# The second half of a layer's columns in one pass: loads by two experts, and four outputs after the last product

## The chip, the core and the metric

The kernel runs on one core of a Trainium2 chip. The core has a matrix engine (TensorE, PE in the rows, with PEld for its weight loads), three engines for elementwise work (VectorE or DVE, ScalarE or ACT, GpSimd or POOL), an engine that issues transfers (SyncE, SP), and 16 DMA engines that move data between the device memory and the on-chip memory. Matrix products are written to PSUM, a small memory that DVE and ACT read out. The metric is device time in microseconds of one execution, lower is better.

## What is computed

An attention between 512 tokens and 32 states of 8 batches and 8 heads gives 8 x 544 rows of 512 columns; a soft mixture of experts follows. Its second half is what matters here:

```python
logits = x @ phi                                  # 4608 rows, 8 experts x 4 slots
d = softmax(logits, over rows);   slot_input = (d.T @ x).reshape(E, 4, 512)
for e in range(8):
    h = np.maximum(slot_input[e] @ w1[e], 0.0)    # 4 x 1024
    slot_out[e] = h @ w2[e]                       # 4 x 512: the second layer
c = softmax(logits, over the 32 slots)
return c @ slot_out                               # 4608 x 512
```

All numbers are 32-bit floats. w1 and w2 are 16 MB each, the output is 9 MB.

## The kernel before

The first part, the attention and the sums over all rows, follows an order written out by hand (ORDER), and is the same in both kernels. After it the kernel runs the first layer of the experts (`w1_part`, h_ps), then the second layer, then the outputs.

**The second layer in column pieces.** The 512 columns of w2 are made in pieces. Columns 0 to 255 are one piece, `wide_part`, whose sum stands in the PSUM tile so[0]; columns 256 to 383 and 384 to 511 are two pieces of 128, `w2_part` with k = 2 and 3, in so[2] and so[3]. For each piece `part` runs over two halves hf of the 1024 hidden features and over 8 experts e: 4 matmuls each, one for each 128 features, into 4 groups of 32 partitions that run side by side. `so_copy(k)` takes the finished piece out of PSUM (ACT the first 128 columns, DVE the rest), `so_sum(k)` adds the 4 groups with a matmul by `rep`, and ACT copies the sum to so_r.

**The outputs.** `out(k, q)` makes 128 of the 512 output columns (k = 0 to 3) for half of the tokens (q): 4 matmuls of so_r with the softmax weights lt_all, 4 copies into a 1 MB tile, by ACT and DVE in turn, and one DMA from SP's queue. `out_by_batches` does the same for (3, 0) in two halves of 512 KB, in PSUM tiles of 256 columns. `out_st(k)` makes 128 columns for the state rows; after each second one a 256 KB DMA, out_s, is issued.

**The order.** The code's order is the order on each engine. At the end (from line 887) small parts stand between the outputs: `more(n)` runs the next n of 32 parts of 128 columns, first all 16 of k = 2, then those of k = 3. out(0, 0) to out(1, 1) need the first piece alone, out(2, *) need k = 2, and out(3, *) need k = 3.

**Loads.** All loads from the third batch on and all outputs go through SP's one queue, in order of issue; SP waits for the buffer of a transfer before it issues it, and for the eighth transfer before it. `load_w` takes weights from a list `todo`. The columns 256 to 511 come in four loads of 2 MB (L117), each with 128 columns of 4 experts; between the second and the third is one load for the first piece, `last`. They use the four `pairs` buffers that the first layer's weights leave. The four are issued before the first layer's second half is done.

Of the kernel before, what the change touches and what calls it, by code (L numbers as in the profile page):

```python
# [8 lines left out]
F32 = mybir.dt.float32  # L9
# [6 lines left out]
P = 128  # L16
# [4 lines left out]
E = 8  # L21
F = 1024
NJ = S // P
# [40 lines left out]
def attention_soft_moe(ctx: ExitStack, tc: tile.TileContext, x0, x1, x, st0, st1, phi, w1, w2a, w2b, out_x, out_s):  # L64
# [6 lines left out]
    nc = tc.nc  # L71
    pe, act, dve, pool = nc.tensor, nc.scalar, nc.vector, nc.gpsimd
# [3 lines left out]
    big = ctx.enter_context(tc.tile_pool(name="big", bufs=NBIG))  # L76
    pairs = ctx.enter_context(tc.tile_pool(name="pairs", bufs=NPAIR))
# [6 lines left out]
    for b in range(B):  # L84
        t = big.tile([P, 4, NJ, 2 * D], F32, tag="big", name=f"x{b}")
# [18 lines left out]
    w1t, w2t = {}, {}  # L104
    todo = [(1, hf, e) for hf in range(2) for e in range(E)]
    todo += [(2, k, e) for k in range(2) for e in range(0, E, 2)]
    last = todo.pop()
    todo += [(3, 0, 0), (3, 0, 4), last, (3, 1, 0), (3, 1, 4)]
    both = []

    def load_w(n):
        for _ in range(min(n, len(todo))):
            layer, k, e = todo.pop(0)
            if layer == 3:
                t = pairs.tile([P, 4 * F], F32, tag="pair", name=f"w3_{k}_{e}")
                t = t.rearrange("p (e k f) -> p e k f", e=4, k=8)
                nc.sync.dma_start(t, w2b[e // 4, k])  # L117
                for i in range(32):
                    w2t[3, k, e + i // 8, i % 8] = t[:, i // 8, i % 8]
                continue  # L120
            if layer == 1 and len(w1t) < 8 * NPAIR:
                if not both:
                    t = pairs.tile([P, 4 * F], F32, tag="pair", name=f"w1_{k}_{e}")
                    both.extend((t[:, 0 : 2 * F], t[:, 2 * F :]))
                t = both.pop(0)
            else:
                t = big.tile([P, 2 * F], F32, tag="big", name=f"w{layer}_{k}_{e}")
            if layer == 1:
                t = t.rearrange("p (k f) -> p k f", k=4)
                nc.sync.dma_start(t, w1[k, e])  # L130
                for i in range(4):
                    w1t[k, e, i] = t[:, i]
            else:
                t = t.rearrange("p (e k f) -> p e k f", e=2, k=4)
                nc.sync.dma_start(t, w2a[e // 2, k])
                for i in range(8):
                    w2t[layer, k, e + i // 4, i % 4] = t[:, i // 4, i % 4]
# [30 lines left out]
    lt_all = cp.tile([P, B, P], F32, name="lt_all")  # L168
# [8 lines left out]
    with ExitStack() as actx:  # L177
        wk = actx.enter_context(tc.tile_pool(name="work", bufs=1))
        sm = actx.enter_context(tc.tile_pool(name="small", bufs=2))
        ps_s = actx.enter_context(tc.tile_pool(name="ps_s", bufs=2, space=PSUM))  # L180
        ps_t = actx.enter_context(tc.tile_pool(name="ps_t", bufs=3, space=PSUM))
        ps_m = actx.enter_context(tc.tile_pool(name="ps_m", bufs=3, space=PSUM))
# [10 lines left out]
        def half(name):  # L193
            return wk.tile([P, S], F32, tag="h", name=name, bufs=NH)

        def mtile(shape, name):
            return ps_m.tile(shape, F32, tag="ms", name=name)
# [467 lines left out]
        def SIe():  # L665
# [5 lines left out]
            E=E_, ee=ee, A=A_, ae=ae, R=R_, sr=sr, srT=srT, srTe=srTe, Lx=Lx, keep=keep, mx=mx, mk=mk,  # L671
# [85 lines left out]
        so, so_sb, so_r = {}, {}, {}  # L757

        def part(k, hf, e, cols, w):
            if hf == 0 and e == 0:  # L760
                so[k] = ps_s.tile([P, cols], F32, tag="sc", name=f"so_ps{k}")
            for i in range(4):
                pe.matmul(  # L763
                    so[k][32 * i : 32 * i + 32, :],
                    h_m[hf][:, 256 * i + 32 * e : 256 * i + 32 * e + 32],
                    w(i),
                    start=(hf == 0 and e == 0),
                    stop=(hf == 1 and e == E - 1),
                )
# [1 line left out]
        def wide_part(hf, e):  # L771
            part(0, hf, e, 256, lambda i: w2t[2, hf, e, i])

        def w2_part(k, hf, e):
            part(k, hf, e, P, lambda i: w2t[3, k - 2, e, 4 * hf + i])

        def so_copy(k):
            cols = so[k].shape[1]
            so_sb[k] = half(f"so_sb{k}")[:, 0:cols]
            act.copy(so_sb[k][:, 0:P], so[k][:, 0:P])  # L780
            if cols > P:
                dve.tensor_copy(so_sb[k][:, P:cols], so[k][:, P:cols])

        def so_sum(k, half_of=0):
            c = slice(P * half_of, P * half_of + P)
            p = mtile([P, P], f"sum_ps{k}_{half_of}")
            pe.matmul(p, rep, so_sb[k][:, c], start=True, stop=True)
            i = k + half_of
            if i % 2 == 0:
                so_r[i // 2] = half(f"so_r{i // 2}")[:, 0:256]  # L790
            act.copy(so_r[i // 2][:, P * (i % 2) : P * (i % 2) + P], p)

        def out(k, q):
            hf, col = k // 2, 128 * (k % 2)
            o = [(ps_t if j % 2 else ps_m).tile([P, 512], F32, tag="tr" if j % 2 else "ms", name=f"o{k}_{q}_{j}")
                 for j in range(NJ)]
            for j in range(NJ):
                rows = slice(32 * j, 32 * j + 32)
                pe.matmul(  # L799
                    o[j],  # L800
                    so_r[hf][rows, col : col + 128],
                    lt_all[rows, 4 * q : 4 * q + 4, :].rearrange("p b s -> p (b s)"),
                    start=True,
                    stop=True,
                )
            ot = big.tile([P, NJ, 512], F32, tag="big", name=f"out{k}_{q}")
            for jp in range(2):
                act.copy(ot[:, 2 * jp, :], o[2 * jp])  # L808
                dve.tensor_copy(ot[:, 2 * jp + 1, :], o[2 * jp + 1])  # L809
            nc.sync.dma_start(out_x[k, q], ot)  # L810

        def out_by_batches(k, q):
            hf, col = k // 2, 128 * (k % 2)
            homes = ((ps_m, "ms"), (ps_t, "tr"), (ps_m, "ms"), (ps_t, "tr"), (ps_s, "sc"), (ps_t, "tr"), (ps_s, "sc"), (ps_m, "ms"))
            o = [h.tile([P, 256], F32, tag=tag, name=f"o{k}_{q}_{i}") for i, (h, tag) in enumerate(homes)]
            ot = big.tile([P, 2, NJ, 256], F32, tag="big", name=f"out{k}_{q}")
            to = out_x[k, q].rearrange("p j s -> (p j s)").rearrange("(i p j s) -> i p j s", i=2, p=P, j=NJ)
            for i in range(2):
                b = 4 * q + 2 * i
                for j in range(NJ):  # L820
                    rows = slice(32 * j, 32 * j + 32)
                    pe.matmul(
                        o[4 * i + j],
                        so_r[hf][rows, col : col + 128],
                        lt_all[rows, b : b + 2, :].rearrange("p b s -> p (b s)"),
                        start=True,
                        stop=True,
                    )
            for i in range(2):
                for jp in range(2):  # L830
                    act.copy(ot[:, i, 2 * jp], o[4 * i + 2 * jp])
                    dve.tensor_copy(ot[:, i, 2 * jp + 1], o[4 * i + 2 * jp + 1])
                nc.sync.dma_start(to[i], ot[:, i])

        ot = []

        def out_st(k):
            rows = slice(32 * k, 32 * k + 32)
            o = mtile([P, 256], f"os{k}")
            pe.matmul(  # L840
                o,
                so_r[k // 2][rows, P * (k % 2) : P * (k % 2) + P],
                lts_all[rows].rearrange("p k i n -> p (k i n)"),
                start=True,
                stop=True,
            )
            if k % 2 == 0:
                ot.append(half(f"out_s{k // 2}"))
            act.copy(ot[-1][:, 256 * (k % 2) : 256 * (k % 2) + 256], o)
            if k % 2:  # L850
                nc.sync.dma_start(out_s[k // 2], ot[-1])
# [26 lines left out]
        for e in range(E):  # L878
            wide_part(1, e)

        rest = [(k, hf, e) for k in (2, 3) for hf in range(2) for e in range(E)]

        def more(n):
            for _ in range(n):
                w2_part(*rest.pop(0))

        so_copy(0)
        more(1)
        so_sum(0)
        more(1)  # L890
        so_sum(0, 1)
        out(0, 0)
        more(5)
        out(0, 1)
        more(5)
        out(1, 0)
        more(4)
        so_copy(2)
        out(1, 1)
        so_sum(2)  # L900
        more(4)
        out_st(0)
        out_st(1)
        out(2, 0)
        more(6)
        out(2, 1)
        more(6)
        so_copy(3)
        out_st(2)
        so_sum(3)  # L910
        out_by_batches(3, 0)
        out_st(3)
        out(3, 1)

# [33 lines left out]
```

## Time and profile before

| what | value |
|---|---|
| median of three runs | 130.05 us (129.82 to 130.21) |
| span of the profiled execution, first to last instruction | 128.2 us |
| TensorE busy in it | 117.7 us (92%) |
| DVE, ACT, POOL busy | 86.7, 76.9, 44.8 us |
| moved by DMA | 51.74 MB, mean 404 GB/s |
| mean granted TensorE clock | 0.980 of full speed |
| last TensorE instruction ends | 120.7 us |

The execution's own time is not listed beside its span; the median of the runs is 1.85 us above the span, and this stands for what lies around it. Shares and rows below are of the one profiled execution, times in microseconds from the start of its span. "Landing" is the time at which the last part of a transfer has reported its end. A transfer is spread over the 16 DMA engines, and the DMA share of a stretch is the mean of the 16; it can go a little above 1 in a short stretch, since a packet is counted where it ends or begins.

### The profile page before, as it was taken

What the parts mean: (1) busy time and instruction counts of PE and PEld (TensorE: products, weight loads), DVE (VectorE), ACT (ScalarE), POOL (GpSimd) and SP (SyncE); (2) the same over time, 40 slices, a digit from 0 to 9 for tenths busy, and PEclk for the clock granted to TensorE, in tenths of its full rate; (3) what the DMA queues carried; (4) which work ended last, traced back from release to release, by engine and by line L of the source; (5) the groups of instructions that cost most, each with busy time, mean ns of one, the idle gap of its engine ahead of it and who ended that gap; (6) DMA issues with size and microseconds to landing.
All of it is one profiled execution on the core that took longest, in us unless ns stands there. A gap on an engine that the chain in (4) does not pass through costs nothing.

```text
span 128.2 us, 4700 instructions
## 1 busy us (share of the span) xinstructions
PE 117.7 (92%) x1992; PEld 81.7 (64%) x1992; DVE 86.7 (68%) x194; ACT 76.9 (60%) x189; POOL 44.8 (35%) x63
## 2 busy tenths in 40 slices
PE   5999999999999999999999999999999999998600
PEld 2857686789795869768767769953465655575200
DVE  2329999999999999999985669019830356442600
ACT  4039999999999999999965711310100436645600
POOL 3004366391947467467882105703500000000000
PEclk9999999999999999999999999999999999999965
DMA  4999999999999999999999999999999989999992
GB/s 125 377 407 430 424 427 422 424 422 424 422 419 422 427 419 429 419 429 417 429 417 435 412 420 402 459 440 409 412 445 445 389 366 417 429 406 422 385 423 100
DMA packets 8373, 51.74 MB, mean 404 GB/s; under 512 B 928, under 2 KB 1184, under 8 KB 3360
## 3 DMA queue, kind: packets, MB, share of 16 engines
q1 hardware_dynamic: 8064, 50.93, 95.5%
q10 hardware_dynamic: 288, 0.52, 1.1%
q8 instruction: 15, 0.25, 0.7%
q14 instruction: 6, 0.05, 0.1%
HBM read 42.53 MB, written 8.91 MB: 401 GB/s over the span
## 4 chain that ended last, share of the span: by engine, by line
PE 71%; DVE 9%; DMA 7%; ACT 5%; issue 1%; POOL 0%; ACTq 0%; DVEq 0%; POOLq 0%
PE so_ps L763 12%; PE h_ps L700 11%; PE xt_ps L229 8%; PE o L799 7%; PE sc L248 5%; DMA phi_sb<-phi_in 5%; PE eT_ps L312 4%; PE sr_ps L346 4%; PE an_ps L312 3%; PE lt L381 3%; DMA x<-x_in 3%; PE t_ps L506 2%; DVE sums L277 2%; DVE q L261 2%; DVE m L266 1%
## 5 line engine op out<-in xcount | busy, mean ns | idle before, releaser
L270 POOL TENSOR_TENSOR q<-q,m 128x512 f32<-128x512 f32 x16 | 16.8, 1050 | 15.7 <-DVE m L266 7.3
L234 ACT ACTIVATE xt<-xt_ps 128x512 f32<-128x512 f32 x30 | 17.9, 618 | 5.9 <-PE xt_ps L229 5.7
L229 PE MATMUL xt_ps<-ident,x 128*128 128x128 f32 x128 | 19.3, 293 | 0.0
L288 POOL TENSOR_TENSOR q<-q,rr 128x512 f32<-128x512 f32 x16 | 16.5, 1051 | 5.1 <-DVE rr L283 3.6
L229 PEld LDWEIGHTS xt_ps<-ident,x 128*128 128x128 f32 x128 | 15.5, 151 | 3.1 <-PE sc L248 0.8
L763 PE MATMUL so_ps<-w,h_m 128*32 128x128 f32 (+1 forms) x384 | 15.7, 310 | 0.0
L763 PEld LDWEIGHTS so_ps<-w,h_m 128*32 128x32 f32 x384 | 10.7, 110 | 7.4 <-issue 4.6
L809 DVE COPY out<-o 128x512 f32<-128x512 f32 x14 | 9.2, 688 | 9.0 <-PE o L799 8.8
L700 PE MATMUL h_ps<-w,si_m 128*32 128x512 f32 x128 | 14.4, 594 | 0.1
L299 DVE TENSOR_REDUCE nm<-sc 128x1 f32<-128x512 f32 x16 | 10.6, 670 | 2.7 <-PE sc L248 2.7
L808 ACT COPY out<-o 128x512 f32<-128x512 f32 x14 | 7.7, 588 | 6.8 <-PE o L799 6.7
L700 PEld LDWEIGHTS h_ps<-w,si_m 128*32 128x32 f32 x128 | 9.1, 110 | 3.9 <-issue 2.9
L304 ACT ACTIVATE e<-sc,nm 128x512 f32<-128x512 f32 x16 | 11.3, 711 | 0.4 <-DVE nm L299 0.3
L261 DVE STREAM_TRANSPOSE q<-sc 128x512 f32<-128x512 f32 x16 | 11.1, 695 | 0.1
L293 DVE STREAM_TRANSPOSE aT<-q 128x512 f32<-128x512 f32 x16 | 10.9, 689 | 0.3 <-POOL q L288 0.2
L266 DVE TENSOR_REDUCE m<-q 128x16 f32<-128x512 f32 x16 | 10.5, 659 | 0.0
L277 DVE TENSOR_REDUCE sums<-q 128x16 f32<-128x512 f32 x16 | 10.4, 664 | 0.1
L273 ACT ACTIVATE q<-q 128x512 f32<-128x512 f32 x16 | 10.4, 650 | 0.1
L346 PE MATMUL sr_ps<-x,eT 128*32 128x64 f32 x512 | 10.4, 220 | 0.0
L312 PE MATMUL eT_ps<-ident,e 128*128 128x128 f32 x64 | 9.8, 279 | 0.0
L248 PE MATMUL sc<-xt,stT_sb 64*32 64x512 f32 x128 | 9.8, 601 | 0.0
L346 PEld LDWEIGHTS sr_ps<-x,eT 128*32 128x32 f32 x512 | 8.6, 110 | 1.3 <-issue 0.8
(124 smaller groups left out, 186.1 us busy)
## 6 DMA issues: line engine op xcount, KB each, us to landing
w<-w_in SPq DMA_DIRECT2D x16, 1024.0 KB, 19.7
w<-w2b_in SPq DMA_DIRECT2D x4, 2048.0 KB, 14.7
out_x<-out SPq DMA_DIRECT2D x7, 1024.0 KB, 6.0
x<-x_in SPq DMA_DIRECT2D x6, 1024.0 KB, 13.5
w<-w2a_in SPq DMA_DIRECT2D x6, 1024.0 KB, 19.4
x<-x_in SPq DMA_DIRECT2D x2, 512.0 KB, 5.9
w<-w2a_in SPq DMA_DIRECT2D x2, 512.0 KB, 12.4
w<-w2a_in SPq DMA_DIRECT2D x4, 256.0 KB, 14.4
```

Of the source, the lines that this page charges most:

```text
L229: pe.transpose(p[:, P * j : P * j + P], xb[b][:, g, j, :], ident)
L234: act.mul(r[f"xt{g}"], r[f"xp{g}"], 0.125)
L248: pe.matmul(r[f"sp{h}"][32 * g : 32 * g + 32, :], st_t(b, g)[64 * h : 64 * h + 64, :], r[f"xt{g}"][64 * h : 64 * h + 64, :], start=True, s ...
L261: dve.transpose(r[f"q{h}"], r[f"sp{h}"])
L266: dve.tensor_reduce(out=r[f"m1{h}"], in_=r[f"qv{h}"], axis=AX.X, op=ALU.max)
L270: pool.tensor_tensor(v, v, R[b][f"m1{h}"].broadcast_to([P, 16, NS]), op=ALU.subtract)
L277: dve.tensor_reduce(out=v, in_=R[b][f"qv{h}"], axis=AX.X, op=ALU.add)
L288: pool.tensor_tensor(v, v, r.broadcast_to([P, 16, NS]), op=ALU.mult)
L312: pe.transpose(p[:, j, :], r[f"{src}{h}"][:, P * j : P * j + P], ident)
L346: pe.matmul(r["srp"][32 * g : 32 * g + 32, h, :], r[f"eT{h}"][:, j, 32 * g : 32 * g + 32], xb[b][:, g, j, D * h : D * h + D], start=(j == ...
L700: pe.matmul(h_ps[hf][32 * kt : 32 * kt + 32, :], si_m[kt // 2][:, 256 * (kt % 2) + 32 * e : 256 * (kt % 2) + 32 * e + 32], w1t[hf, e, kt], ...
L763: pe.matmul(so[k][32 * i : 32 * i + 32, :], h_m[hf][:, 256 * i + 32 * e : 256 * i + 32 * e + 32], w(i), start=(hf == 0 and e == 0), stop=( ...
```

## The change

The columns 256 to 511 become one piece of 256 columns, as the first half is. Its four loads of 2 MB hold two experts each with all 256 columns, instead of four experts with 128. Its 16 parts of 256 columns run expert by expert, both halves of the features of an expert in turn, so that they use the loads in their order. The first four outputs stand between the parts, after 2, 5, 8 and 10 of them; all 16 parts come before `so_copy(2)`, and out(2, 0), out(2, 1), out(3, 0) and out(3, 1), 1 MB each, follow the two sums of the second piece. `out_by_batches` is gone: out(3, 0) is made by `out`, in one transfer. out_st(0) and out_st(1) come ahead of the sums, out_st(2) and out_st(3) ahead of the last output.

```diff
-    todo += [(3, 0, 0), (3, 0, 4), last, (3, 1, 0), (3, 1, 4)]
+    todo += [(3, 0, 0), (3, 0, 2), last, (3, 0, 4), (3, 0, 6)]
...
             if layer == 3:
-                t = pairs.tile([P, 4 * F], F32, tag="pair", name=f"w3_{k}_{e}")
-                t = t.rearrange("p (e k f) -> p e k f", e=4, k=8)
-                nc.sync.dma_start(t, w2b[e // 4, k])
-                for i in range(32):
-                    w2t[3, k, e + i // 8, i % 8] = t[:, i // 8, i % 8]
+                t = pairs.tile([P, 4 * F], F32, tag="pair", name=f"w3_{e}")
+                t = t.rearrange("p (e k f) -> p e k f", e=2, k=8)
+                nc.sync.dma_start(t, w2b[e // 2])
+                for i in range(16):
+                    w2t[3, e + i // 8, i % 8] = t[:, i // 8, i % 8]
...
-        def w2_part(k, hf, e):
-            part(k, hf, e, P, lambda i: w2t[3, k - 2, e, 4 * hf + i])
+        def second_part(hf, e):
+            part(2, hf, e, 256, lambda i: w2t[3, e, 4 * hf + i])
...
-        rest = [(k, hf, e) for k in (2, 3) for hf in range(2) for e in range(E)]
+        rest = [(hf, e) for e in range(E) for hf in range(2)]
...
         out(0, 0)
-        more(5)
+        more(3)
         out(0, 1)
-        more(5)
+        more(3)
         out(1, 0)
-        more(4)
+        more(2)
+        out(1, 1)
+        more(6)
         so_copy(2)
-        out(1, 1)
-        so_sum(2)
-        more(4)
         out_st(0)
         out_st(1)
+        so_sum(2)
+        so_sum(2, 1)
         out(2, 0)
-        more(6)
         out(2, 1)
-        more(6)
-        so_copy(3)
+        out(3, 0)
         out_st(2)
-        so_sum(3)
-        out_by_batches(3, 0)
         out_st(3)
         out(3, 1)
```

The array w2b is laid out on the host to match, 16 KB for each partition of a load in both kernels.

On TensorE, from out(1, 1) to out(2, 0): before, with so_ps the products, sum_ps the sums, os those of out_st and o those of out (h_m_1665 and h_m_1666 are the two halves of the hidden features, so_r_1877 and so_r_2002 the two halves of the columns):

```order
L799 MATMUL o_1_0_1986<-lt_all,so_r_1877 128x512
L799 MATMUL o_1_1_1987<-lt_all,so_r_1877 128x512
L799 MATMUL o_1_2_1988<-lt_all,so_r_1877 128x512
L799 MATMUL o_1_3_1989<-lt_all,so_r_1877 128x512
L787 MATMUL sum_ps_0_2000<-so_sb_1984,rep 128x128
L763 MATMUL so_ps_2004<-w_1_0_1731,h_m_1665 32x128 x16
L840 MATMUL os_2021<-lts_all,so_r_1877 128x256
L840 MATMUL os_2025<-lts_all,so_r_1877 128x256
L799 MATMUL o_0_0_2029<-lt_all,so_r_2002 128x512
L799 MATMUL o_0_1_2030<-lt_all,so_r_2002 128x512
L799 MATMUL o_0_2_2031<-lt_all,so_r_2002 128x512
L799 MATMUL o_0_3_2032<-lt_all,so_r_2002 128x512
```

and in the changed kernel, from the last of out(1, 1)'s matmuls on (so_r_2011 is the second half of the columns):

```order
L799 MATMUL o_1_3_1963<-lt_all,so_r_1877 128x512
L763 MATMUL so_ps_1870<-w_4_1731,h_m_1665 32x256 x4
L763 MATMUL so_ps_1870<-w_4_1731,h_m_1666 32x256 x4
L763 MATMUL so_ps_1870<-w_6_1733,h_m_1665 32x256 x4
L763 MATMUL so_ps_1870<-w_6_1733,h_m_1666 32x256 x4
L763 MATMUL so_ps_1870<-w_6_1733,h_m_1665 32x256 x4
L763 MATMUL so_ps_1870<-w_6_1733,h_m_1666 32x256 x4
L817 MATMUL os_2001<-lts_all,so_r_1877 128x256
L817 MATMUL os_2005<-lts_all,so_r_1877 128x256
L787 MATMUL sum_ps_0_2009<-so_sb_1998,rep 128x128
L787 MATMUL sum_ps_1_2013<-so_sb_1998,rep 128x128
L799 MATMUL o_0_0_2016<-lt_all,so_r_2011 128x512
```

Ahead of out(2, 0) stood one sum, four small parts of the third piece and out_st; now the last six wide parts, out_st and both sums stand there.

On ACT, at the same place, before (so_sb is the copy of so_copy, so_r that of the sum):

```order
L780 COPY so_sb_1984<-so_ps_1870 128x128
L808 COPY out_1_1994<-o_1_0_1986 128x512
L808 COPY out_1_1994<-o_1_2_1988 128x512
L791 COPY so_r_2002<-sum_ps_0_2000 128x128
L849 COPY out_s_2023<-os_2021 128x256
L849 COPY out_s_2023<-os_2025 128x256
L808 COPY out_0_2037<-o_0_0_2029 128x512
```

and in the changed kernel:

```order
L808 COPY out_1_1968<-o_1_0_1960 128x512
L808 COPY out_1_1968<-o_1_2_1962 128x512
L780 COPY so_sb_1998<-so_ps_1870 128x128
L826 COPY out_s_2003<-os_2001 128x256
L826 COPY out_s_2003<-os_2005 128x256
L791 COPY so_r_2011<-sum_ps_0_2009 128x128
L791 COPY so_r_2011<-sum_ps_1_2013 128x128
L808 COPY out_0_2024<-o_0_0_2016 128x512
```

The copy of the second piece's sum, so_r, stood ahead of the two out_s copies and now stands behind them, and so_copy(2) comes after out(1, 1)'s copies.

## Rows read from the trace of the kernel before

**Rows 1.** The page: span, and DMA share in 40 slices, in tenths.

```profile
span 128.2 us, 4700 instructions
...
DMA  4999999999999999999999999999999989999992
```

**Rows 2.** Windows: stretch, length, busy per engine, clock, DMA share, GB/s.

```profile
103.00:104.00 1.00, 1.00 (x16) 0.24 (x15) 0.10 (x1) 0.14 (x1) 0.00 (x0) 1.00 0.73 287
...
105.00:118.00 13.00, 12.64 (x221) 7.65 (x218) 5.45 (x9) 6.41 (x16) 0.00 (x0) 1.00 1.02 422
...
119.00:120.00 1.00, 1.00 (x7) 0.30 (x4) 0.56 (x3) 0.67 (x3) 0.00 (x0) 1.00 0.71 295
...
125.00:126.00 1.00, 0.00 (x0) 0.00 (x0) 0.00 (x0) 0.00 (x0) 0.00 (x0) 0.50 0.60 254
126.00:127.00 1.00, 0.00 (x0) 0.00 (x0) 0.00 (x0) 0.00 (x0) 0.00 (x0) 0.50 0.10 41
```

**Rows 3.** SP's issues (timeline): first start, length of all, line, transfer, count.

```profile
84.82 0.90 SPq L117 DMA_DIRECT2D w<-w2b_in  x2
102.96 7.01 SPq L810 DMA_DIRECT2D out_x<-out  x4
110.99 0.33 SPq L851 DMA_DIRECT2D out_s<-out_s  x1
112.72 3.43 SPq L810 DMA_DIRECT2D out_x<-out  x2
...
121.44 0.33 SPq L810 DMA_DIRECT2D out_x<-out  x1
```

**Rows 4.** Issue to landing: two last loads, first output, out_s, out(2, 0).

```profile
DMA to landing us min/median/max: 16.2/18.3/20.4
...
DMA to landing us min/median/max: 5.8/5.8/5.8
...
out_s<-out_s SPq DMA_DIRECT2D x1, 256.0 KB, 5.7
...
out_x<-out SPq DMA_DIRECT2D x1, 1024.0 KB, 6.4
```

**Rows 5.** Chain that ended last (start, us, what), and timeline rows of the first output.

```profile
93.45 5.36 PE so_ps L763 x96
...
99.21 0.49 PE sum_ps L787 x2
99.70 0.36 PE so_ps L763 x8
...
100.47 1.07 PE o L799 x8
101.54 1.23 PE so_ps L763 x40
...
120.68 0.69 DVE out L809
...
100.40 1.14 PE L799 MATMUL o<-lt_all,so_r 32*128 32x512 f32 x8
...
101.61 1.29 DVE L809 COPY out<-o 128x512 f32<-128x512 f32 x2 [2.12 <-PE o L799]
```

**Rows 6.** Timeline of TensorE and ACT around out_st and the last sum.

```profile
109.59 0.70 PE L840 MATMUL os<-lts_all,so_r 32*128 32x256 f32 x4
...
110.32 0.65 ACT L849 COPY out_s<-os 128x256 f32<-128x256 f32 x2 [0.83 <-PE os L840]
...
116.91 0.27 ACT L791 COPY so_r<-sum_ps 128x128 f32<-128x128 f32 x1
117.23 0.74 PEld L822 LDWEIGHTS o<-lt_all,so_r 32*128 32x128 f32 x16 [0.55 <-ACT so_r L791]
```

**Rows 7.** Windows of a quarter microsecond, columns as in rows 2.

```profile
103.75:104.00 0.25, 0.25 (x12) 0.23 (x12) 0.10 (x1) 0.14 (x1) 0.00 (x0) 1.00 1.53 557
...
126.75:127.00 0.25, 0.00 (x0) 0.00 (x0) 0.00 (x0) 0.00 (x0) 0.00 (x0) 0.50 0.00 0
```

## What was predicted

> **What bounds the kernel now.** I read the page first: the span is 128.2 us, and the DMA row stands at 9 in nearly every slice from the second to the last but one [rows 1]. TensorE looks as full there, so the question is which of them sets the end. The end of the chain and the timeline settle it: TensorE is done at 120.7 us, the last copy into an output tile at 121.4, when the last output is issued [rows 3, 5]; what is left, to 127.2 us, is transfer. From 105 to 118 us the DMA share is 1.02, at 422 GB/s [rows 2].
>
> Next I strung the landings of the end together, issue plus time to landing, last part of each [rows 3, 4] (the row of 6.4 us stands for the fourth output and for out(2,0), one each, and that of 5.8 for the first and the last). The last 2 MB weight load lands at 85.3 + 20.4 = 105.7 us, the first output at 103.0 + 5.8 = 108.8, the fourth at 109.6 + 6.4 = 116.0, the 256 KB out_s at 111.0 + 5.7 = 116.7, out(2,0) at 112.7 + 6.4 = 119.1, and the last output at 121.4 + 5.8 = 127.2. From the first to the fourth it is 2.4 us for 1 MB, from out(2,0) to the last 8.1 us for 3.25 MB, 2.5 each: the slowest of the 16 DMA engines is never without work. The span ends 1.0 us after that landing. The others do run dry: the share is 0.73 from 103 to 104, while the last load is still under way, 0.71 from 119 to 120, and it fades over 1.5 us at the end (0.60, then 0.10) [rows 2]. So some engines lead the slowest by about 1.5 us, and the end is that of the slowest.
>
> An output issued too late for the slowest engine moves the end by its whole lateness; one issued earlier moves nothing. The question about the change is therefore: when is each output issued, against when the queue needs it.
>
> **The change part by part.** *Loads.* The bytes, the number of DMAs, their order on SP's queue and the buffers that they wait for stay; only which weights lie in each 2 MB does. Zero, as long as they are there in time. The first of the two late loads (experts 4 and 5) was the 16.2 us one of the pair, landing at 84.8 + 16.2 = 101.0, the second at 105.7 [rows 4]. By the chain below they are first needed at 106.5 and 109.4 us: 3.7 us of cover at the least.
>
> *Products.* Before, 32 parts of 128 columns; after, 16 parts of 256. Five small parts take 1.23 us in the chain (40 instructions, 8 a part), so 0.246 each; twelve wide ones take 5.36 us, so 0.447 each [rows 5]. TensorE saves 32 x 0.246 - 16 x 0.447 = 7.87 - 7.15 = 0.7 us of work. But none of it is worth anything by itself, since TensorE ends 6.5 us before the last landing; what counts is the order.
>
> *The first four outputs.* Both kernels end the first piece's products at 93.45 + 5.36 = 98.82 us. From there, by the chain's durations: the first part now takes 0.45 and holds the sum to 99.27 (before 99.21); the second takes 0.45 where 0.36 stood; out(0,0) starts at 100.6, 0.15 later than the chain's 100.47 [rows 5]. Then out 1.07, three parts 1.34 (five small ones took 1.23), out 1.07, three parts 1.34, out 1.07, two parts 0.89 (four small ones took 4 x 0.246 = 0.98): out(0,1) starts at 103.0, out(1,0) at 105.4, out(1,1) at 107.4, which is 0.15 to 0.4 us later than before. From the start of such matmuls to the issue it is 102.96 - 100.40 = 2.56 us, as DVE's two copies end at 101.61 + 1.29 [rows 3, 5]. The slowest engine finishes its last load's bytes about 0.45 us ahead of the landing, at 105.25, and the first output's bytes reach it at about 104; 0.15 us later is hidden, and with outputs coming every 2.4 us, or a little faster, the next three keep pace with 2.4 us of transfer each. Cost 0.
>
> *The last four outputs.* Here the order changes most. Before, out(2,0) needed half of the small parts and was issued at 112.72, long before its turn. Now all 16 parts come first. The chain goes on: out(1,1) ends at 107.4 + 1.07 = 108.5, six parts 2.68, so the product is complete at 111.15. Then so_copy(2), two out_st matmuls (0.63, TensorE free at 111.8), the two sums. ACT sits in the middle: its first out_s copy starts 110.32 - 109.59 = 0.73 us after the out_st matmuls, and two of them take 0.65 [rows 6], so to 112.5; only then come so_r's copy (0.27) and the gap of 0.04 to the matmuls that read it [rows 6]. The sum, 0.49 us, is ready for that copy at 112.3, so it waits 0.2 us for ACT, behind the two out_s copies. out(2,0) starts at 112.9 and is **issued at 112.9 + 2.56 = 115.4 us**, 2.7 us later than before.
>
> When is it needed? The time from issue to first byte is not a row of its own. The first output was issued at 102.96, with engines dry; the share, 0.73 over that whole microsecond, is 1.53 in its last quarter [rows 2, 7], so its bytes start about 0.85 us after the issue. From the last byte to the landing: the share is gone by 126.75, the landing is at 127.2 [rows 3, 4, 7], 0.45 us. The slowest engine has its part of out_s done at 116.7 - 0.45 = 116.25, and out(2,0) arrives there at 115.4 + 0.85 = 116.25. **It comes just in time for the slowest engine**, and up to 1.5 us late for those that lead. The lead was never worth anything at the end; the change spends it. By this sum out(2,0) lands at 116.25 + 2.45 + 0.45 = 119.15 against 119.1.
>
> Bounds for this time from issue to landing with nothing queued: at most 5.8 us, by the first output, which stood behind the last load on some engines [rows 4]; at least 2.45, the transfer. I take 0.85 + 2.45 + 0.45 = 3.75, since it is read from the same transfer on engines that were dry. With 5.8 the landing is at 121.2 and the end 2.1 us later; with 2.45 nothing changes.
>
> A fixed time of 2.0 us beside bytes over 436 GB/s stands in the Trainium skill, "DMA: Bandwidth & Descriptors", section "Anatomy of one DMA", for another issuing path; by it 1 MB takes 4.4 us, an estimate, and out(2,0) would land at 119.8. The rows here put 1.3 us beside the transfer, and I go by them.
>
> *After that.* out(2,1), out(3,0) and out(3,1) need no further product. DVE's copies pace them, 1.29 us each, so they are issued near 116.8, 118.1 and 119.7 (ACT's two out_s copies lie between), while the queue wants one each 2.45 us: always ahead. From out(2,0)'s landing to the last it was 127.2 - 119.1 = 8.1 us, with the same bytes; one 1 MB transfer in place of two of 512 KB is the same bytes, and the spacing of 2.5 us a megabyte there is the same as elsewhere. The late dip at 119 to 120 goes, for engines that did not set the end.
>
> **Sum.** The last landing comes at 119.15 + 8.1 = 127.25 instead of 127.2. Slips of the TensorE and ACT chain now show one for one where they go above zero, and earliness is lost, so I add 0.1. The span becomes 128.35. Spans leave out what lies around them: the profiled execution's span is 128.2, the three runs of the kernel have a median of 130.05, 1.85 more. Forecast: 130.05 + 0.15 = **130.2 us**.
>
> **The rivals.**
> *The chain is late.* TensorE needs more than 0.447 for a wide part between other work, or ACT and the sums take longer than placed; then all 16 engines run dry before out(2,0). It decides from 115.4 us on, and each 0.1 us later costs 0.1. If wide parts cost two small ones, 0.49, fourteen of them add 0.6 us, and the time is 130.65 to 130.8. For it: the chain is eleven steps long, and each handover can cost more. Against: the chain of before adds up from the same steps without idle pieces between them [rows 5]. Chance 0.20.
> *The empty queue takes longer to start and end.* Halfway between my 3.75 us and the bound of 5.8, out(2,0) lands 1.0 us later, and the time is 131.2; at the bound it is 132.2. For it: the whole landing of the first output is above my value [rows 4]. Against: the quarter from 103.75 shows data 0.85 us after the issue [rows 7]. Chance 0.13. By the Trainium skill's fixed time, named above, it would be 0.65 us later, 130.85.
> *The tail's gaps close.* The dips of 103 to 104 and of 119 to 120 are 0.27 + 0.29 = 0.56 us of all engines' time [rows 2]. Were the end set by bytes over all engines instead of by the slowest one, the earlier issues after out(2,0) would win back the second dip, 0.3 us, and the time would be 129.7. Against: landings 2.4 to 2.5 us apart to the end, and the first dip stays. Chance 0.07.
> *The change doesn't do what it says*, with experts 6 and 7 arriving after their products are due: 3.7 us of cover speak against it; it would be slower by what exceeds them. Chance 0.02, counted as slower.
>
> **How the numbers follow.** The forecast, 129.9 to 130.45, has what is left, 0.58. About 0.3% (0.4 us) is what a measurement of this kernel can tell from no change. Of the rivals, the late chain and the slow start are slower by over 0.3% nearly whole, 0.32 with a lost load; the closing gaps, at 0.35 us, are divided between faster and the same. Faster 0.07, same 0.60, slower 0.33. The range runs from 129.75, most of the gap case, to 131.1, which takes in the late chain and nearly half of the slow start; what lies above, towards the bound of 5.8 us, is left out.
>
> **What would show it.** In the profile of the changed kernel: so_ps 16 parts near 0.45 us, done near 111.15; out(2,0) issued near 115.4, not 112.7; a dip of the DMA share between 114.5 and 116.5, deep but short of zero; the dip near 119 to 120 gone; no fade of 1.5 us at the end, but engines that end together; the last landing about 11.8 us after out(2,0)'s issue. It is wrong if out(2,0) is issued after 115.8, if the share goes to zero for longer than 0.3 us, or if the last landing comes before 127.0.

## The result, and the profile after

| what | before | after |
|---|---|---|
| median of five runs | 130.05 us (129.59 to 130.36) | 130.93 us (130.85 to 131.05) |
| ratio to before, 95% interval | | 1.0068 (1.0043 to 1.0093) |
| span of the profiled execution | 128.2 us | 129.1 us |
| out(2,0) issued | 112.72 | 115.71 |
| last landing | 127.2 | 128.2 |

The change makes the kernel 0.9 us slower. The forecast was 130.2 us, the range 129.75 to 131.1 holds the measured time, and slower by over 0.3% had a chance of 0.33: the likeliest case was not the one that came.

The page of the changed kernel (span, and the DMA share in 40 slices):

```profile
span 129.1 us, 4422 instructions
...
DMA  4999999999999999999999999999999889969993
```

A 6 stands near the end where the kernel before had 9 [rows 1]. The windows of that stretch and of the end (columns as in rows 2):

```profile
114.00:115.00 1.00, 1.00 (x9) 0.27 (x3) 0.67 (x2) 0.71 (x2) 0.00 (x0) 1.00 0.84 336
115.00:116.00 1.00, 1.00 (x10) 0.95 (x9) 1.00 (x3) 0.85 (x2) 0.00 (x0) 1.00 0.37 150
116.00:117.00 1.00, 1.00 (x11) 0.77 (x6) 0.98 (x3) 0.92 (x2) 0.00 (x0) 1.00 0.68 285
117.00:118.00 1.00, 1.00 (x10) 0.65 (x9) 1.00 (x2) 0.98 (x4) 0.00 (x0) 1.00 0.93 393
125.00:126.00 1.00, 0.00 (x0) 0.00 (x0) 0.00 (x0) 0.00 (x0) 0.00 (x0) 0.50 0.98 416
126.00:127.00 1.00, 0.00 (x0) 0.00 (x0) 0.00 (x0) 0.00 (x0) 0.00 (x0) 0.50 0.93 393
127.00:128.00 1.00, 0.00 (x0) 0.00 (x0) 0.00 (x0) 0.00 (x0) 0.00 (x0) 0.50 0.05 16
...
127.00:127.25 0.25, 0.00 (x0) 0.00 (x0) 0.00 (x0) 0.00 (x0) 0.00 (x0) 0.50 0.11 33
127.25:127.50 0.25, 0.00 (x0) 0.00 (x0) 0.00 (x0) 0.00 (x0) 0.00 (x0) 0.50 0.08 33
127.50:127.75 0.25, 0.00 (x0) 0.00 (x0) 0.00 (x0) 0.00 (x0) 0.00 (x0) 0.50 0.00 0
```

From 105 to 118 us the share was 1.02 before [rows 2]. Now 0.16, 0.63 and 0.32 us of all engines' time are missing from 114 to 117: the engines run dry one after another and wait for out(2,0). At the end the picture is turned round too. Before, the share faded over 1.5 us (0.60, then 0.10); now it stays at 0.93 to 127, and after that only 8 KB are begun in each of two quarters (33 GB/s for 0.25 us). In the trace's list of packets these are two of 8 KB, begun at 127.14 and 127.45 us, 0.309 us each, one behind the other: the rest of one engine's share. The lead of some engines is gone, as forecast, and one straggler is left, which was not.

SP's issues (start, length, line, transfer, count), and the time to landing of out(2,0), issued at 115.71, and of the last output, issued at 120.26:

```profile
103.21 7.41 SPq L810 DMA_DIRECT2D out_x<-out  x4
112.93 0.33 SPq L828 DMA_DIRECT2D out_s<-out_s  x1
115.71 2.84 SPq L810 DMA_DIRECT2D out_x<-out  x3
...
120.26 0.98 SPq L810 DMA_DIRECT2D out_x<-out  x1
...
DMA to landing us min/median/max: 3.9/3.9/3.9
...
DMA to landing us min/median/max: 8.0/8.0/8.0
```

out(2,0) lands at 115.71 + 3.9 = 119.6 us, where it was 119.1 [rows 3, 4], and the last output at 120.26 + 8.0 = 128.2, where it was 127.2. So 0.5 us is lost up to out(2,0)'s landing, and another 0.5 between it and the end: 8.6 us for the same 3.25 MB that took 8.1.

The chain of waits on the way there (start, us, what), and ACT's copy of the sum in the timeline:

```profile
99.74 0.57 PE so_ps L763 x8
...
101.79 1.43 PE so_ps L763 x24
...
106.80 1.00 PE so_ps L763 x16
107.80 1.07 PE o L799 x8
108.87 2.73 PE so_ps L763 x48
111.60 0.63 PE os L817 x4
112.23 0.42 PE sum_ps L787 x2
...
113.17 4.07 PE o L799 x22
...
112.79 0.68 ACT L791 COPY so_r<-sum_ps 128x128 f32<-128x128 f32 x2
```

### The profile page after: what moved, and what is told of

It is laid out like the page before. It is cut to its first block, busy times and chain, and to the rows that moved or that the text cites. A ratio compares the mean times of both kernels' runs of the same rounds, so it can differ in the third digit from the quotient of the medians.

```text
span 129.1 us, 4422 instructions
## 1 busy us (share of the span) xinstructions
PE 116.1 (90%) x1856; PEld 78.8 (61%) x1856; DVE 86.7 (67%) x193; ACT 76.2 (59%) x186; POOL 44.7 (35%) x63
## 4 chain that ended last, share of the span: by engine, by line
PE 69%; DVE 9%; DMA 8%; ACT 5%; issue 1%; DVEq 0%; POOL 0%; ACTq 0%; POOLq 0%
PE so_ps L763 11%; PE h_ps L700 11%; PE xt_ps L229 8%; PE o L799 7%; DMA phi_sb<-phi_in 5%; PE sc L248 5%; PE sr_ps L346 4%; PE eT_ps L312 4%; PE an_ps L312 3%; PE lt L381 3%; DMA x<-x_in 3%; PE t_ps L506 2%; DVE sums L277 2%; DVE q L261 2%; PE sum_ps L787 1%; DVE m L266 1%
## 5 line engine op out<-in xcount | busy, mean ns | idle before, releaser
L229 PEld LDWEIGHTS xt_ps<-ident,x 128*128 128x128 f32 x128 | 15.0, 148 | 3.2 <-PE sc L248 0.8
L809 DVE COPY out<-o 128x512 f32<-128x512 f32 x16 | 10.2, 685 | 8.4 <-PE o L799 8.4
L763 PE MATMUL so_ps<-w,h_m 128*32 128x256 f32 x256 | 15.2, 381 | 0.0
L763 PEld LDWEIGHTS so_ps<-w,h_m 128*32 128x32 f32 x256 | 7.7, 110 | 8.2 <-issue 3.8
L808 ACT COPY out<-o 128x512 f32<-128x512 f32 x16 | 8.5, 589 | 6.2 <-PE o L799 6.2
L799 PE MATMUL o<-lt_all,so_r 32*128 32x512 f32 x64 | 10.2, 636 | 0.0
## 6 DMA issues: line engine op xcount, KB each, us to landing
w<-w2a_in SPq DMA_DIRECT2D x2, 512.0 KB, 12.5
```

Of the source, the lines that this page charges most:

```text
L229: pe.transpose(p[:, P * j : P * j + P], xb[b][:, g, j, :], ident)
L763: pe.matmul(so[k][32 * i : 32 * i + 32, :], h_m[hf][:, 256 * i + 32 * e : 256 * i + 32 * e + 32], w(i), start=(hf == 0 and e == 0), stop=( ...
L799: pe.matmul(o[j], so_r[hf][rows, col : col + 128], lt_all[rows, 4 * q : 4 * q + 4, :].rearrange("p b s -> p (b s)"), start=True, stop=True,)
```

## The experiments

Two theories came out of this. **Theory 1:** the loss is out(2,0)'s lateness for the DMA engines, and nothing else of the change costs anything. **Theory 2:** the part of the loss that arises after out(2,0)'s landing is the straggler: an engine that also fetches a piece of a program ends behind the others, once no engine has a lead in which to hide it. The rivals are named with each run. All ratios are to the kernel before, run beside on the same chip.

**out(2,0) early again, all else as changed.**

```diff
-        more(6)
+        del rest[:5]
+        more(1)
         so_copy(2)
```

> The changed kernel without five of the last six wide parts (their share of the sum is left out), all loads and outputs as before. Theory 1 (the change costs what out(2,0) is late for the DMA engines): the product is done 5 x 0.45 = 2.2 us sooner, out(2,0) is issued near 113.5 instead of 115.7 us, ahead of its due point of about 115.3, and the time is that of the kernel before, 130.05 us, ratio 1.000 (0.998 to 1.002). Rival (the new layout of the loads, the order of the products by expert, or out(3,0) in one transfer costs by itself): the time stays near 130.9, ratio 1.007.

Measured: 130.04 us, ratio 0.9986 (0.9965 to 1.0007). SP issues out(2,0) at 113.62 us, and the windows show no hole (timeline, then windows):

```profile
113.62 2.93 SPq L810 DMA_DIRECT2D out_x<-out  x3
...
114.00:115.00 1.00, 1.00 (x11) 0.74 (x5) 0.98 (x3) 1.00 (x3) 0.00 (x0) 1.00 1.04 420
115.00:116.00 1.00, 1.00 (x9) 0.68 (x8) 1.00 (x2) 0.98 (x4) 0.00 (x0) 1.00 1.04 430
```

The loads by two experts, the order by expert (with 11 of the 16 parts) and the whole out(3,0) are all in this kernel, and it has the time of the kernel before. They cost nothing that can be measured; the whole loss hangs on when out(2,0) comes.

**out(2,0) later still.**

```diff
-        more(6)
+        rest[5:5] = rest[0:5]
+        more(11)
         so_copy(2)
```

> The changed kernel with five of the last six wide parts done twice (so their share counts twice in the output). Theory 1: out(2,0) is issued 2.2 us later, near 117.9 us, all engines are dry, and the time rises one for one, to 130.9 + 2.2 = 133.1 us, ratio to the kernel before 1.024. Rival: TensorE's work is hidden behind transfers and the time stays near 130.9, ratio 1.007.

Measured: ratio 1.0227 (1.0199 to 1.0255). Against the changed kernel's 1.0068 that is 1.6%, or 2.1 us, for five parts more, which are 5 x 0.43 = 2.15 us by the slope found below. Within the intervals, which leave some 0.5 us on either side, lateness beyond the changed kernel's counts one for one.

**The kernel before, with out(2,0) moved back.** The loads, the small parts and the split out(3,0) are as before; only the order at the end is another.

```diff
-        out(2, 0)
-        more(6)
-        out(2, 1)
-        more(6)
+        more(12)
+        out(2, 0)
+        out(2, 1)
```

> The kernel before with its own loads, parts and split out(3,0); only out(2,0) and out(2,1) are moved behind the last twelve small parts. Theory 1: out(2,0) is issued 2 x 1.45 = 2.9 us later than at 112.7, near 115.6, like in the changed kernel, and the time is that of the changed kernel, 130.5 to 131.0 us, ratio 1.004 to 1.007. Rival (layout or the one transfer of out(3,0) costs): 130.05, ratio 1.000.

Measured: 131.27 us, ratio 1.0083 (1.0058 to 1.0107). The issues and the hole, as in the changed kernel (timeline, then windows):

```profile
103.16 7.01 SPq L810 DMA_DIRECT2D out_x<-out  x4
...
115.76 1.63 SPq L810 DMA_DIRECT2D out_x<-out  x2
...
114.00:115.00 1.00, 1.00 (x9) 0.22 (x3) 0.62 (x2) 0.66 (x2) 0.00 (x0) 1.00 0.81 330
115.00:116.00 1.00, 1.00 (x7) 0.66 (x6) 1.00 (x3) 0.90 (x2) 0.00 (x0) 1.00 0.40 160
116.00:117.00 1.00, 0.59 (x5) 0.19 (x2) 0.96 (x2) 0.87 (x3) 0.00 (x0) 1.00 0.67 279
```

The kernel before, given the same issue time, loses the same. With only half of that move,

```diff
-        out(2, 0)
         more(6)
+        out(2, 0)
         out(2, 1)
```

> The kernel before with out(2,0) moved behind six of the last twelve small parts, out(2,1) right after it. Theory 1: out(2,0) is issued near 114.2 us, still before its due point of about 115.3, so nothing changes: 130.05 us, ratio 1.000 (0.998 to 1.002). If each 0.1 us of lateness cost 0.1 from the start, without slack, it would be 131.5, ratio 1.011.

it measured 129.9 us, ratio 0.9991 (0.9971 to 1.001) (timeline, then the time from out(2,0)'s issue to its landing):

```profile
103.38 7.01 SPq L810 DMA_DIRECT2D out_x<-out  x4
114.66 1.63 SPq L810 DMA_DIRECT2D out_x<-out  x2
...
DMA to landing us min/median/max: 5.0/5.0/5.0
```

out(2,0) is issued at 114.66 there, 1.9 us later than before; but the first output of this execution came 0.4 us later too, so against it out(2,0) is 1.5 us later. It takes 5.0 us to land where the dry queue took 3.9, so it still found work ahead of it. Counted the same way, from the first output, out(2,0) is 2.7 us later than before in the changed kernel and 2.8 in the run with all twelve products ahead of it. The slack is real: 1.5 us of delay cost nothing, 2.7 to 2.8 us cost 0.9 to 1.1. The prediction's due point, 115.4, lies 2.7 us after the old issue; the runs don't place it more exactly. These four runs settle theory 1.

**What fills the queue counts, not the chain alone.**

```diff
-        out_st(0)
-        out_st(1)
         so_sum(2)
         so_sum(2, 1)
         out(2, 0)
+        out_st(0)
+        out_st(1)
```

> The changed kernel with out_st(0) and out_st(1) behind out(2,0). out(2,0) is issued about 0.3 us sooner, near 115.4, since ScalarE's two out_s copies no longer stand ahead of the sum's copy. Theory 1 says still that it is no gain: the 256 KB out_s, whose transfer of 0.65 us filled the queue ahead of out(2,0), now comes behind it, so the engines are dry 0.65 us sooner, and the end moves by 0.65 - 0.3 = +0.3 us: 131.2, ratio 1.009. Rival (only TensorE's and ScalarE's chain to out(2,0) counts, not what fills the queue meanwhile): the time falls by 0.3 us to 130.6, ratio 1.004.

Measured: 131.35 us, ratio 1.0081 (1.0056 to 1.0106). out(2,0) is issued sooner, as forecast, and lands in the same 3.9 us; out_s follows it, and the engines stand still for longer (timeline, windows):

```profile
115.44 0.33 SPq L810 DMA_DIRECT2D out_x<-out  x1
115.91 0.34 SPq L828 DMA_DIRECT2D out_s<-out_s  x1
...
114.00:115.00 1.00, 0.76 (x7) 0.33 (x3) 0.91 (x2) 0.95 (x2) 0.00 (x0) 1.00 0.41 172
115.00:116.00 1.00, 1.00 (x10) 0.73 (x10) 0.38 (x1) 0.77 (x3) 0.00 (x0) 1.00 0.04 16
```

The share from 114 to 116 is 0.41 and 0.04 where the changed kernel has 0.84 and 0.37. A ratio of 1.004, by which only the chain would count, is outside the interval; whether it is worse than the changed kernel, as expected, the overlapping intervals leave open. So it is no gain that out(2,0) is issued 0.3 us sooner: out_st ahead of the sums, where the change put it, holds ACT up but fills the queue.

**One part of the change alone:** in the kernel before, out_by_batches(3, 0) is replaced by out(3, 0), and the host's reordering of it goes.

> The kernel before with one part of the change alone: out(3,0) made by out in one transfer of 1 MB instead of two of 512 KB. Its issue moves from 118.9 (first half) to about 117.2 + 2.6 = 119.8 us. Theory 1: the slowest engine has its part of out(2,1) done at 121.6 - 0.45 = 121.15, so its due point is 121.15 - 0.85 = 120.3, and nothing changes: 130.05, ratio 1.000 (0.998 to 1.003). Rival (an issue later by 0.9 us, or bigger packets, costs at once): 130.5 to 131, ratio 1.004 to 1.007.

Measured: 130.14 us, ratio 0.9988 (0.9968 to 1.0009). No cost, no gain.

**The straggler.** In the changed kernel's trace a fetch of 8 KB by the instruction queue q14 falls at 119.9 us (queue rows of the stretch 119.8 to 120.0: packets, MB, share):

```profile
q1 hardware_dynamic: 6, 0.05, 57.9%
q14 instruction: 1, 0.01, 9.7%
```

It is the only such fetch after 114 us, and lies after the moment at which all engines had been dry. The trace also has the time at which each of a transfer's 16 parts, one for each engine, reports its end, and that tells whether the straggler and the fetch go together (times in us; the rows between are runs from above, the last row is the last run below):

| kernel | fetch | out(2,0), first and last part | last output, first part | 15th | last |
|---|---|---|---|---|---|
| before | 119.9 | 117.09, 119.15 | 125.63 | 127.15 | 127.20 |
| before, out(2,0) behind six more products | 119.0 | 118.32, 119.61 | 126.42 | 127.52 | 127.58 |
| before, behind twelve more products | 119.9 | 119.43, 119.63 | 127.45 | 127.62 | 128.46 |
| changed | 119.9 | 119.37, 119.59 | 127.36 | 127.53 | 128.21 |
| changed, out_st behind | 120.6 | 119.10, 119.33 | 127.76 | 127.93 | 128.61 |
| changed, four more issues of SP | 115.0 | 119.31, 119.99 | 127.49 | 127.95 | 127.97 |

In the changed kernel the parts of out(2,0) land within 0.22 us. From out(2,1) on, which lands between 121.81 and 122.05 but for one part at 122.67, one part comes 0.6 to 0.7 us behind the other 15: one engine fell back just where the fetch stands. The packets say by how much. One of 8 KB takes 0.309 us, as the fetch does. Of the packets that join the fetch without a gap, each begun where the one ahead of it ends, those begun at 119.16 and 120.22 us took 0.440 and 0.451 us. In sum that engine lost 0.58 us. The two other kernels whose engines all start out(2,0) together, with the fetch behind that start, have the same lone part, 0.7 to 0.8 us late. In the kernel before, and with six more products ahead, out(2,0)'s parts are 1.3 to 2.1 us apart, and the fetch leaves no lone part at the end.

Whose program is it? Two runs add 20 tiny instructions to VectorE and to ScalarE, where these are idle:

```diff
                 h_turn(1)
                 h_relu(1)
+                spare = cp.tile([P, 20], F32, name="spare")
+                for i in range(20):
+                    dve.tensor_copy(spare[:, i : i + 1], mask[:, 0:1])
```

> The changed kernel with 20 tiny VectorE copies (128x1) after the second h_relu, near 95 us, where VectorE has nothing to do until 99. Theory 2: once all 16 DMA engines wait for out(2,0), none has a lead left, and the one that also fetches an 8 KB piece of a program at 119.9 us ends 0.65 us behind the other 15 and sets the end. If it is VectorE's program, 20 more instructions move this fetch to where VectorE stood 20 instructions earlier, before 110 us, where leads remain: the last landing comes 11.8 instead of 12.5 us after out(2,0)'s issue, and the time falls by 0.65 us, from 130.9 to 130.25, ratio 1.002. If it is another engine's program, or the straggler has another cause, nothing changes: 130.9, ratio 1.007.

With act.copy in its place:

> The changed kernel with 20 tiny ScalarE copies (128x1) at the same place, where ScalarE has nothing to do until 98.9 us. Theory 2, if the piece of program fetched at 119.9 us is ScalarE's: the fetch moves before 111 us and the time falls by 0.65 us to 130.25, ratio 1.002. If it is VectorE's or another's: 130.9, ratio 1.007.

Measured: 131.57 us, ratio 1.0108 (1.0072 to 1.0145), and 131.38 us, 1.0083 (1.0055 to 1.0111). In both the fetch stays, at 120.0 to 120.4 us; it is neither engine's. Both read slower than the changed kernel (1.0068), though the intervals overlap. The kernel before with the same 20 VectorE copies shows a reason:

> The kernel before with the same 20 tiny VectorE copies. Theory 2: there the fetch at 119.9 us falls on an engine with a lead over the slowest, so moving it changes nothing: 130.05, ratio 1.000 (0.998 to 1.002). If the fetch cost the kernel before 0.6 us too, the time falls to 129.45, ratio 0.995; if the copies themselves cost something, it rises in both kernels alike.

Measured: 131.2 us, ratio 1.0066 (1.0041 to 1.0092). It rises, as the last case of that text has it, but not by that cause: the rate of the loads fell, long before the copies run. The windows from 20 to 85 us, of the kernel before and of this one:

```profile
20.00:85.00 65.00, 64.24 (x1232) 50.36 (x1216) 55.21 (x127) 51.84 (x134) 35.60 (x46) 1.00 1.01 423
```

```profile
20.00:85.00 65.00, 63.83 (x1229) 50.37 (x1216) 55.56 (x128) 52.05 (x134) 35.73 (x46) 1.00 1.02 418
```

The added tile has 80 bytes per partition, and tiles placed behind it would move. Two runs divide the tile from the copies: one tiny copy into the same tile, and 20 copies into a tile of 128 bytes.

> The kernel before with a tile of 80 bytes per partition and one tiny VectorE copy instead of 20. Theory 3: all of b_dve20's loss is there, ratio 1.0066 (1.004 to 1.009), packets of 16 KB at a mean of 618 ns. Rival (the 20 copies cost): ratio 1.000.

Measured: 131.0 us, ratio 1.0065 (1.0044 to 1.0085), 418 GB/s from 20 to 85 us.

> The kernel before with the same 20 tiny VectorE copies as b_dve20, but into a tile of 128 bytes per partition instead of 80, so that every tile that is placed after it moves by 128 bytes instead of 80. Theory 3 (an 80 byte shift of the tiles makes each DMA packet longer: 618 against 613 ns for 16 KB in that trace, 418 against 423 GB/s from 20 to 85 us): packets are back at 611 to 613 ns and the time is 130.05, ratio 1.000 (0.998 to 1.002). Rival (the 20 copies themselves cost 0.9 us): ratio 1.0066 as in b_dve20.

Measured: 131.06 us, ratio 1.007 (1.0049 to 1.009), again 418 GB/s. So the 20 copies are not the cause, but a tile of 128 bytes costs as much as one of 80: an alignment to 128 bytes does not explain it. An alignment to 256 bytes, of which neither size is a multiple, would; no run tests it. What remains is that a tile more in this place, with at least one instruction that uses it, costs 0.65 to 0.7%, over the whole of the loads; why, these runs don't tell. It is not the chip: the run with out(3,0) in one transfer was made on the same one beside the last two, and its loads run at 424 GB/s. It also means that the two runs with 20 tiny instructions in the changed kernel carry this cost, and against the changed kernel are no test of the time that the straggler takes.

The last run gives SP four issues more, between the last load and the first output:

```diff
                 h_turn(1)
                 h_relu(1)
+                spare = cp.tile([P, 32], F32, name="spare")
+                for i in range(4):
+                    nc.sync.dma_start(spare[0:1, 8 * i : 8 * i + 8], phi[0:1, 0, 0:8])
```

> The changed kernel with four tiny DMAs of 32 bytes (one DMA engine) issued by SP between the last load and the first output, and a 128 byte tile for them. Theory 2, if the piece of program fetched at 119.9 us is SP's own: four more DMA issues move this fetch four issues forward, before 113 us, where some engines still have a lead; the last landing then comes 11.8 to 11.9 us after out(2,0)'s issue, no engine ends alone 0.65 us after the others, and the time falls from 130.9 to 130.3, ratio 1.002. If the fetch is not SP's it stays near 119.9 us: 130.9, ratio 1.007.

Measured: 130.87 us, ratio 1.0067 (1.004 to 1.0093). The fetch has moved: q14 has its packet between 114.5 and 115.5 us, and none from 115.5 to 128, when all has landed (queue rows of these two stretches):

```profile
q1 hardware_dynamic: 65, 0.23, 57.1%
q14 instruction: 1, 0.01, 2.0%
...
q1 hardware_dynamic: 796, 4.69, 90.6%
```

In the changed kernel it falls behind the second out_s and ahead of the last output; here it falls behind the first out_s and ahead of out(2,0), four issues of SP earlier: it is SP's own program. out(2,0) is issued at 115.60, the last output, issued at 120.13, lands 7.8 us later, at 127.97, and no engine is left alone at the end (share 1.00 from 126 to 127, 0.41 and 0.16 in the next two quarters, then nothing):

```profile
126.00:127.00 1.00, 0.00 (x0) 0.00 (x0) 0.00 (x0) 0.00 (x0) 0.00 (x0) 0.50 1.00 418
127.00:127.25 0.25, 0.00 (x0) 0.00 (x0) 0.00 (x0) 0.00 (x0) 0.00 (x0) 0.50 0.41 164
127.25:127.50 0.25, 0.00 (x0) 0.00 (x0) 0.00 (x0) 0.00 (x0) 0.00 (x0) 0.50 0.16 66
127.50:128.00 0.50, 0.00 (x0) 0.00 (x0) 0.00 (x0) 0.00 (x0) 0.00 (x0) 0.50 0.00 0
```

But the expected 130.3 us did not come. This kernel has a tile more as well, its loads run at 418 GB/s, and a tile alone cost 0.65 to 0.7% in the three kernels above; its out(2,0) takes 4.4 us to land. From out(2,0)'s issue to the last landing it is 12.4 us, against 12.5 in the changed kernel, at a rate that is 1.4% lower. The fair comparison is with the two runs that carry the tile and keep the fetch: there it is 12.55 and 12.57 us, and the times are 131.57 and 131.38 us where this run has 130.87. That points the way of theory 2, by 0.2 us in the traces and 0.5 to 0.7 in the times, but the intervals of the ratios overlap. With the tile the lone part is no clean sign either: out(2,0)'s parts are 0.5 to 0.9 us apart in these three runs, and of the two that keep the fetch one ends with a lone part 0.36 us late, the other with four late ones. So the runs show that the fetch is SP's, and the traces without the tile that it sets its engine back by 0.6 us and that this engine ends last; what moving it is worth in time no run shows clear of the noise.

No kernel of these beats both. The best are at the time of the kernel before.

## Why the prediction was right and wrong

**What bounds the kernel: right.** The end follows the slowest DMA engine. 1.5 us of delay for out(2,0) cost nothing, 2.7 to 2.8 us cost about 1, and five parts more cost what they take.

**Loads, order of the products, out(3,0) in one: right.** Their cost of nothing is shown by the run that has all three and an early out(2,0), though it leaves out five parts, and by out(3,0) alone.

**The first four outputs: right.** They are issued 0.25 to 0.65 us later than before (103.21 against 102.96 for the first; the four issues span 7.41 us where they spanned 7.01 [rows 3]), a little more than the forecast 0.15 to 0.4, and up to 114 us the queue does not run dry over it.

**The chain to out(2,0): the first mis-sized term.** Forecast 115.4, measured 115.71. The price of a wide part was taken from a stretch of twelve [rows 5], as a plain multiple. The rows after give 1.00 for two, 1.43 for three and 2.73 for six: 0.43 for each part and about 0.13 for each new stretch after other matmuls. The old stretch of small parts had such a start in it as well: five took 1.23 us, but one alone 0.36 [rows 5], and the prediction divided the 1.23 by five. With five stretches between other work the product was done at 111.60 instead of 111.15. On ACT 0.2 us of that came back: the copy of the sum was forecast at 112.5 and began at 112.79, and out(2,0)'s matmuls began at 113.17 where 112.9 was forecast. This is the rival of the late chain, with a price of 0.3 us.

**The time from issue to landing: nearly right.** 3.75 us was forecast, 3.9 measured, in four kernels with dry engines, and 4.2 to 4.6 in the three that carry a tile more; the bound of 5.8 was far too high, since that transfer stood behind loads. The Trainium skill, "DMA: Bandwidth & Descriptors", section "Anatomy of one DMA", gives 2.0 us beside the transfer, for another issuing path, an estimate of 4.4 us for 1 MB; these traces show 3.9, and by that about 1.45 beside a transfer of 2.45.

**From out(2,0) to the end: the step that failed.** The prediction took 8.1 us over from the kernel before, and said of the engines' lead that it "was never worth anything at the end; the change spends it". It is 8.6 us now. By the table above 15 engines need 7.9 us, where all 16 need 8.0 in the kernel before and with six more products ahead of out(2,0); one comes 0.7 us behind them. What the prediction left out is a transfer that is none of the kernel's data: SP's fetch, which costs its engine 0.6 us. In the kernel before the fetch fell at the same time, 119.9 us, when some engines were dry (0.71 from 119 to 120 [rows 2]), and the end shows nothing of it. That a lead hid it there is the reading of the traces; no run moved the fetch in that kernel.

So the last landing was forecast at 127.25 us. The late chain makes that 127.55, and there 15 engines are done (127.53); the straggler's 0.7 us make it 128.2. The chain was among the slips that "show one for one where they go above zero", for which 0.1 us was added; the straggler was under no term and no rival. The prediction's other signs fit this: the dip of the DMA share came deep but short of zero (0.37), and the last landing came 11.8 us after out(2,0)'s issue for 15 engines and 12.5 us for the last.

In the one execution shown, the queue ahead of out(2,0) was 0.2 us later as well (out_s lands at 116.9 where it was 116.7). Executions differ by that much, so the split of the 1.0 us holds to about 0.2.

**The chances.** Same had 0.60 on a sum that put the arrival and the due point on the same quarter of a microsecond. When the margin is zero, an error that makes the chain later costs and one that makes it earlier gains nothing, so slower should have had the greater share. That the range held is in part luck: it reached to 131.1 us for a late chain and a slow start of the empty queue, and of these only 0.3 us came; the rest is the straggler.

## What to carry to other kernels

In a kernel that ends with transfers, write a due point beside each output: the landing of what is ahead of it in the queue, less the time from issue to first byte and from last byte to landing. An output delayed by less than its slack cost nothing (1.5 us here); beyond it the delay shows in the time. A sum that ends at a margin of zero should be forecast as a loss, because handovers between stretches of matmuls add up (0.13 us each here, of which ACT gave back less than half). Uneven DMA engines can also be a reserve: by these traces a program fetch on one engine left no mark while the parts of a transfer were 1.3 to 2.1 us apart, and set the end once a wait had brought all of them level.

## What the runs showed of the hardware that was not expected

- A small tile more (80 or 128 bytes per partition) made the loads 1.2% slower, 418 instead of 423 GB/s from 20 to 85 us, in all six kernels that had it; in three of them, otherwise the kernel before, the time was 0.65 to 0.7% longer, with 1 or 20 instructions that use the tile. The cause stays open; a probe that adds a tile should be measured against one that adds the tile alone.
- SP, which only issues transfers, has its program fetched too: a piece of 8 KB, once in the last 15 us here, by one of the DMA engines that move the outputs. It set that engine back by 0.58 us, 0.31 for the piece and 0.27 on two packets around it.
- A stretch of four-way matmuls of 256 columns costs 0.43 us for each part, and 0.13 us once when other matmuls came before it.
